# Attention and MLP on one core: the QKV lead as two streams of 64-row matmuls, with the sync queue in program order

## The chip, the cores and the metric

One core of a Trainium2 chip. The time is that of one launch of the whole program in device microseconds; before the change it is 1637.77 us, the median of three runs (1637.33 to 1638.07).

## The reference

One block of 2048 tokens, width 512, 32 heads of 16, and an MLP of width 1792. Everything is fp32, x has one batch.

```
xn = layernorm(x)                                   # no gain, no bias
q, k, v = split(xn @ wqkv)                          # 32 heads of 16
p  = softmax(q k^T / 4)                             # 2048 x 2048 for each head
s  = concat(p v) @ wo
g  = silu( relu(xn @ w1 + b1)^2 @ w2 + b2 )
return x + s * g
```

## The kernel before, in words

**Precision.** Each operand of a projection is held as a high and a low part, and each product is made of three matmuls, high by high, high by low and low by high (`terms3`, L270). A projection tile of 128 x 512 over a depth of 512 is therefore 12 matmuls: four slices of depth by three terms. A matmul that uses all 128 rows of the array is called full here. A matmul that uses rows 0 to 63 or 64 to 127 is called a half; two halves on different lanes (lane 0 the upper rows, lane 1 the lower ones) run side by side, as a pair. In the records a full matmul has the tile form 128*128 and a half has 64*128.

**Attention.** Heads go in quads, queries in chunks of 512: 8 quads by 4 chunks are 32 units. A unit has 16 blocks of 128 keys, so there are 512 slots. For each slot and each of four heads there is one half matmul of scores and one exponential (`exp_mm`, L1234 on PE and L1246 on ACT), and two slots later four matmuls of probabilities times values into one bank (`pv_mm`, L373). The exponential needs the row maximum, so a first pass computes the same scores with queries on the partitions and takes maxima (`max_mm`, matmul L298, VectorE reduction L305): 4 of these to a slot and 128 to a unit. They run 24 slots (LEAD) ahead of the exponentials. When a unit's maxima are done, `max_end` reduces them once more (L325), and `shift` (L333) turns, negates and splits them on VectorE (L335, L337, L338), stores them to HBM (`keep`, L344) and loads them into rows of the query tiles (`back`, `shift_rows`, L364), where the score matmul subtracts them.

**Lanes.** Heads 0 and 2 of a quad lie on lane 0, heads 1 and 3 on lane 1. The dense work of the MLP and of the output projection is cut into half matmuls too (`halves` L210, `block` L242), so that in the main loop each pair has one dense half on one lane and a maximum or a score on the other. A slot without dense work pairs maxima with scores.

**Start.** Up to 60 us, x is loaded, normalised, transposed and split, and the first projection tiles are made. From there a lead fills the 24 slots of advance with maxima: 48 rounds of one pair of maxima, and after every third pair two full projection tiles, 24 matmuls (`pump(24)`). `qk_tile` (L967) makes a tile of Q or K for eight heads and 512 tokens: 12 matmuls (L972), an evacuation by ACT into `raw` (L996, two buffers), a split by POOL into `hl` (L83 and L84, three buffers), and two stores of 256 KB by SP (L927). `v_tile` (L1011) makes V: matmuls L1019, ACT L1025, one store L1028. The tiles of the first eight heads (`m % 4 == 0`) are split by VectorE straight from the bank instead. The lead also stores the normalised x for the MLP (`xn_d`, L1221, eight stores of 1 MB on odd steps g below 16), and at g = 16 asks for the first MLP weights (L438), the values of quad 0 (L160) and the biases b1 and b2 (L1217, L1218).

**Banks.** PSUM has eight banks: three `se` (pool `pe`), three `pm_t` (pool `pm`), one `pd_t` and one `po`. Projection tiles of the lead alternate between `pd_t` and `po`.

**After the lead.** Slots 0 and 1 each do four maxima and four exponentials around the last projection tile, slots 2 and 3 do the same without it, and from slot 4 the dense work runs in groups of four slots (`long_slots`). The first of its operands is `xc` (L486), a load of 2 x 512 KB of normalised x that takes the place of the projection operands, so it is issued after the last projection matmul. Slots 452 and 453 lie between MLP and output projection and have no dense work; the maxima end with slot 487.

**What sets the order.** Up to the main loop ACT, VectorE and POOL run in program order; PE and SP are ordered by the scheduler of the tile framework. In the loop SP is in program order as well. A store or load deferred by `later(n, ...)` is issued n ticks later; in the loop a tick is a slot.

Of the kernel before, what the change touches and what calls it, by code (L numbers as in the profile page):

```python
# [36 lines left out]
GAPS = (18, 19, 20, 22)  # L37
EPS = 1e-5
# [3 lines left out]
def kernel(  # L42
# [56 lines left out]
    with ExitStack() as ph:  # L99
# [184 lines left out]
        togo = {}  # L284
# [4 lines left out]
        def max_mm(g, j, bank=None):  # L289
            u = g // 16  # L290
            qd = u // 4
            if u not in mxs:
                mxs[u] = sp.tile([P, 16, 4], F32, name="mx")
                for i in range(2):
                    togo[u, i] = [(p, qb, kc) for p in range(2) for qb in range(4) for kc in range(4)]
            p, qb, kc = togo[u, j].pop(0)
# [12 lines left out]
        def max_end(g):  # L309
            u, s = divmod(g, 16)  # L310
# [22 lines left out]
        def shift(u):  # L333
# [26 lines left out]
        in_loop = []  # L360
# [606 lines left out]
        def qk_tile(m, c, last=False):  # L967
            ps = pd.tile([P, 512], F32, name="pd_t") if last else qkv_bank()
# [9 lines left out]
            if last:  # L978

                hl = pools["n"].tile([P, 2, 512], F32R, name="hl")  # L980
                raw = sp.tile([P, 512], F32, name="ot", bufs=1)
                nc.scalar.activation(raw, ps, AF.Copy)
                split((hl[:, 0], hl[:, 1]), raw)
                later(6, lambda: qk_store(m, c, hl))
                yield
                return

            quick = m % 4 == 0 and not hold[0]

            def evac():  # L990
                hl = hlp.tile([P, 2, 512], F32R, name="hl")
                if quick:
                    split_psum(hl[:, 0], hl[:, 1], ps)
                else:
                    raw = hlp.tile([P, 512], F32, name="raw", bufs=2)
                    nc.scalar.activation(raw, ps, AF.Copy)  # L996
                    split((hl[:, 0], hl[:, 1]), raw)
                qk_store(m, c, hl)

            when_done(evac)  # L1000
            yield

# [8 lines left out]
        def v_tile(c, tt):  # L1011
            xT = xTs[c]
            ps = qkv_bank()
            ts_ = slice(tt * P, (tt + 1) * P)
            for out_, lh, rh, first_, last_ in terms3(ps, [
                (lambda a, q, ko=ko: xT[q, a, ko, ts_], lambda b, q, ko=ko: wa_t[q, b, ko, 2 * P :])
                for ko in range(KO)
            ]):
# [4 lines left out]
            def evac():  # L1023
                vt = vts[(4 * c + tt) % NVT]
                nc.scalar.activation(  # L1025
                    vt[:, :, :DH], ps.rearrange("p (h d) -> p h d", d=DH), AF.Copy
                )
                nc.sync.dma_start(v_d[:, c * 4 + tt, :], vt.rearrange("p h d -> p (h d)"))  # L1028

            when_done(evac)  # L1030
            yield
# [46 lines left out]
        rest = []  # L1078

# [10 lines left out]
        vts = [wqa.tile([P, H, VW], F32, name=f"vt{i}") for i in range(NVT)]  # L1090
        first = ExitStack()
# [20 lines left out]
        for i in range(NT + 3):  # L1112
# [38 lines left out]
            if i >= 7 and (i - 3) % 4 == 3:  # L1151
                c = (i - 3) // 4
                ahead.append(qk_tile(4, c))
                rest.append(qk_tile(0, c))
            if i >= 3 and (i - 3) % 4 == 3:
                c = (i - 3) // 4
                rest += [v_tile(c, tt) for tt in range(4)]
        let_go()
# [15 lines left out]
        for n in (2, 3):  # L1174
            fill_ring("ka", n, 1.0)
        rest += [
            qk_tile(m, c, (m, c) == (7, 3)) for c in range(4) for m in (1, 5, 2, 6, 3, 7)
        ]

        pump(47)  # L1180
        led.append(0)
        pump(24)
# [43 lines left out]
        def exp_mm(st, j, pts, spare):  # L1226
            u, kb = divmod(st, 16)
            qd = u // 4
            b = 64 * (j % 2)
            if spare:  # L1230
                se = pm.tile([P, 512], F32, name="pm_t")
            else:
                se = pe.tile([P, 512], F32, name="se")
            nc.tensor.matmul(  # L1234
                se, kas[qd, j // 2][b : b + 64, kb * P : (kb + 1) * P],
                qes[u][j // 2][b : b + 64, :],
                start=True, stop=True,
            )

            oldest_first("pt")  # L1240
# [223 lines left out]
```

## Time and profile before

| what | value |
|---|---|
| median of 3 runs | 1637.77 us |
| span of the profiled execution | 1635.6 us |
| time outside that span (median less span) | about 2.2 us |
| PE busy in it | 1620.8 us, 99% |
| VectorE, ACT, POOL busy | 1356.8, 1189.9, 523.0 us |
| the chain that ended last | PE 99%, VectorE 1% |

The page and the views of the trace give times in microseconds from the start of the span. A row of a timeline has the start, the length, the engine, the line of the kernel, the operation, what it writes and reads, how many instructions were put together in the row and, in brackets, how long its engine stood idle before it and what released it. PE is the matmul, PEld the load of its weights, and SPq the issue of a DMA on the queue of the sync engine SP. Matmuls overlap in the pipeline, so the distance between two starts is a matmul's cost, not the length in its row.

### The profile page before, as it was taken

To read this page: it belongs to the slowest core of one execution; us is meant where nothing else is said; L and a number is where in the kernel's file an instruction comes from. 1 tells how busy PE (TensorE), PEld (TensorE's weight loads), DVE (VectorE), ACT (ScalarE), POOL (GpSimd) and SP (SyncE) were. 2 spreads that over 40 slices of the span, in tenths; PEclk is the share of its full clock that TensorE was granted. 3 is DMA by queue.
4 is the path that set the end of the run, shared out by engine and by line. 5 is a ranking of instruction groups with operands and counts; after the bars stand their busy time and mean duration, and the time that the engine had idled before them with its cause. 6 is when DMAs were issued, how large, how long until landed. Compare 5 with 4: busy or idle time off the path is not lost.

```text
span 1635.6 us, 35352 instructions
## 1 busy us (share of the span) xinstructions
PE 1620.8 (99%) x13300; PEld 923.2 (56%) x13300; DVE 1356.8 (83%) x2345; ACT 1189.9 (73%) x2351; POOL 523.0 (32%) x547
## 2 busy tenths in 40 slices
PE   8999999999999999999999999999999999999998
PEld 6777565456546655664466456645654565445543
DVE  6356888888888888888888888888888888887754
ACT  7311777777777777877777777777777777777786
POOL 6446568123112311321133112311321233125421
PEclk9999999999999999999999999999999999999999
DMA  8768655434333333434343334323532353246654
GB/s 299 193 210 276 205 171 145 125 100 124 83 95 100 109 93 81 129 87 112 79 121 89 83 90 141 101 68 88 147 98 61 88 144 81 60 130 195 193 170 155
DMA packets 164418, 209.18 MB, mean 128 GB/s; under 512 B 59928, under 2 KB 78872, under 8 KB 162712
## 3 DMA queue, kind: packets, MB, share of 16 engines
q1 hardware_dynamic: 163960, 206.40, 44.5%
q8 instruction: 105, 1.72, 0.5%
q14 instruction: 65, 0.53, 0.1%
q10 hardware_dynamic: 288, 0.52, 0.1%
HBM read 149.95 MB, written 56.61 MB: 126 GB/s over the span
## 4 chain that ended last, share of the span: by engine, by line
PE 99%; DVE 1%; DMA 0%; issue 0%; ACT 0%; POOL 0%; DVEq 0%; POOLq 0%
PE po L373 31%; PE pd_t L242 18%; PE pm_t L298 18%; PE se L1234 15%; PE pd_t L210 6%; PE pd_t L972 2%; PE po L972 2%; PE se L1019 1%; PE se L972 1%; PE pd_t L1019 1%; PE se L298 1%; PE po L1019 1%; PE pm_t L1234 1%; PE pm_t L1065 0%; PE pm_t L811 0%; DVE mx L305 0%
## 5 line engine op out<-in xcount | busy, mean ns | idle before, releaser
L305 DVE TENSOR_REDUCE mx<-pm_t 128x1 f32<-128x512 f32 x2000 | 1245.1, 684 | 167.8 <-PE pm_t L298 77.3
L1246 ACT ACTIVATE pt<-se 128x512 f32<-128x512 f32 x2002 | 1044.2, 617 | 257.6 <-PE se L1234 214.5
L298 PE MATMUL pm_t<-ka,qm 64*128 64x512 f32 x2000 | 793.7, 420 | 1.5 <-DVE mx L305 1.3
L1234 PE MATMUL se<-qe,ka 64*128 64x512 f32 x2002 | 674.0, 396 | 0.2 <-ACT pt L1246 0.2
L373 PE MATMUL po<-pt,v 128*32 128x512 f32 x4096 | 545.3, 604 | 0.0
L298 PEld LDWEIGHTS pm_t<-ka,qm 64*128 64x128 f32 x2000 | 350.1, 184 | 244.8 <-DVE mx L305 230.7
L242 PEld LDWEIGHTS pd_t<-xc,w1s 64*128 64x128 f32 x2688 | 334.0, 187 | 93.9 <-issue 88.9
L242 PE MATMUL pd_t<-xc,w1s 64*128 64x256 f32 x2688 | 380.2, 288 | 0.0
L1234 PEld LDWEIGHTS se<-qe,ka 64*128 64x128 f32 x2002 | 337.6, 184 | 20.7 <-ACT pt L1246 2.6
L242 PE MATMUL pd_t<-w2t,hT 64*128 64x512 f32 x1080 | 300.6, 410 | 0.0
L242 PEld LDWEIGHTS pd_t<-w2t,hT 64*128 64x128 f32 x1080 | 179.1, 184 | 80.5 <-issue 75.5
L529 POOL TENSOR_TENSOR r<-r 128x512 f32<-128x512 f32 x56 | 58.2, 1040 | 374.9 <-ACT r L526 374.9
L373 PEld LDWEIGHTS po<-pt,v 128*32 128x32 f32 x4096 | 81.0, 108 | 158.8 <-issue 136.4
L548 POOL TENSOR_TENSOR u<-u,b_t 128x512 f32<-128x512 f32 x16 | 20.6, 1287 | 316.3 <-ACT u L547 316.3
L411 POOL TENSOR_TENSOR ot<-ot,hl 128x512 f32<-128x512 f32 x31 | 39.8, 1284 | 204.4 <-DMA hl<-r_d 91.1
L210 PE MATMUL pd_t<-wot,oc 64*128 64x512 f32 x336 | 90.9, 406 | 0.0
L526 ACT ACTIVATE r<-pd_t,b_t 128x256 f32<-128x256 f32 x112 | 46.9, 470 | 57.1 <-PE pd_t L242 57.1
L210 PEld LDWEIGHTS pd_t<-wot,oc 64*128 64x128 f32 x336 | 58.4, 184 | 45.4 <-ACT pt L1246 14.2
L84 POOL TENSOR_TENSOR hT<-r,hT 128x512 fp32r<-128x512 f32 x56 | 72.2, 1290 | 4.7
L210 PE MATMUL pd_t<-w2t,hT 64*128 64x512 f32 x264 | 68.8, 393 | 0.0
L305 DVE TENSOR_REDUCE mx<-se 128x1 f32<-128x512 f32 x48 | 32.9, 685 | 40.0 <-PE pm_t L298 30.0
L210 PEld LDWEIGHTS pd_t<-w2t,hT 64*128 64x128 f32 x264 | 47.0, 184 | 6.0
(129 smaller groups left out, 928.5 us busy)
## 6 DMA issues: line engine op xcount, KB each, us to landing
w1s<-w_d SPq DMA_DIRECT2D x196, 256.0 KB
qm<-q_d SPq DMA_DIRECT2D x384, 32.0 KB
ka<-k_d SPq DMA_DIRECT2D x96, 128.0 KB
qe<-q_d SPq DMA_DIRECT2D x384, 32.0 KB
xn_d<-xT SPq DMA_DIRECT2D x8, 1024.0 KB
k_d<-hl SPq DMA_DIRECT2D x32, 256.0 KB
q_d<-hl SPq DMA_DIRECT2D x32, 256.0 KB
xc<-xn_d SPq DMA_DIRECT2D x16, 512.0 KB
```

Source lines behind the costliest of these rows:

```text
L84: (lo or nc.gpsimd).tensor_tensor(dst[1], raw, dst[0].bitcast(F32), op=ALU.subtract)
L210: mm = nc.tensor.matmul(out_, lh(r), rh(r), start=first_ and lane == 0, stop=last_ and lane == 1, skip_group_check=True,)
L242: mm = nc.tensor.matmul(out_, lh(r), rh(r), start=first_ and lane == 0, stop=last_ and lane == 1, skip_group_check=True,)
L298: nc.tensor.matmul(ps, qms[u][p][64 * j : 64 * j + 64, qb * P : (qb + 1) * P], kas[qd, p][64 * j : 64 * j + 64, kc * 512 : (kc + 1) * 512] ...
L305: return nc.vector.tensor_reduce(mxs[u][:, c, kc : kc + 1], ps, axis=AX.X, op=ALU.max)
L373: nc.tensor.matmul(po[32 * j : 32 * j + 32, :], vs[qd][:, (4 * kb + j) * VW : (4 * kb + j) * VW + 32], pts[j], start=(kb == 0), stop=(kb = ...
L526: nc.scalar.activation(r[:, i], ps[:, i * CW : (i + 1) * CW], AF.Relu, bias=b1_t[:, fo : fo + 1])
L529: nc.gpsimd.tensor_tensor(r, r, r, op=ALU.mult)
L972: nc.tensor.matmul(out_[:, n0:n1], lh(slice(0, P)), rh(slice(0, P))[:, n0:n1], start=first_, stop=last_,)
L1019: nc.tensor.matmul(out_, lh(slice(0, P)), rh(slice(0, P)), start=first_, stop=last_)
L1234: nc.tensor.matmul(se, kas[qd, j // 2][b : b + 64, kb * P : (kb + 1) * P], qes[u][j // 2][b : b + 64, :], start=True, stop=True,)
L1246: return nc.scalar.activation(pts[j], se, AF.Exp, scale=0.25)
```

## The change

- The lead is rewritten (`side_tile`, `side_rounds`, `lead_rounds`). Tile v(2,0) is made full before it. The other 32 projection tiles are made of halves: 31 in sequence, each on lane 0 and, 18 rounds later, on lane 1 into the same bank, and tile (3,3) "across", on lane 1 in the first 18 rounds and on lane 0 in the last 18, so that both lanes are busy all the time. That is 390 rounds, and between them 60 extra pairs: 51 of two maxima, 9 of a maximum and a score. Six maxima on lane 1 at the head and three scores and three maxima on lane 0 at the tail fill the rest.
- The lead holds 120 maxima and 12 exponentials (slots 0, 1 and 2). Slots 0 and 1 are gone (FIRST = 2), slots 2, 3, 452 and 453 (TWO) hold two maxima each, and the maxima end before slot 486.
- Tiles of the lead lie in `pm_t`, and every fourth in `pd_t`; each bank comes up again four tiles later. All Q and K tiles but the across one go by ACT and POOL.
- SP is in program order in the lead. Stores of tiles are deferred by `later(1)` (V) and `later(2)` (Q, K), with a tick of six rounds; those of (7,3) go to the main loop.
- The stores of `xn_d` are on every third step g up to 23. The block at g = 16 is where it was.
- The loads of query tiles for maxima are asked for at steps 5 and 7 of a unit, not 9 and 11. A unit's last reduction follows the 64th maximum of a lane, and its shift is due six steps later.

```
+FIRST = 2
+LAST_MAX = 486
+TWO = (2, 3, 452, 453)
+ROUND_MM = [12 * k for k in range(1, 32)] + [12 * k + 6 for k in range(2, 22)]
+ROUND_MS = [12 * k + 6 for k in (22, 23, 25, 26, 28, 29)]
+ROUND_SM = [12 * k + 6 for k in (24, 27, 30)]
...
         def max_end(g):
+            for u in [u for u, n in left.items() if n == 0]:
+                del left[u]
+                m4 = m4s[u % 2]
+                nc.vector.tensor_reduce(m4[:, :16], mxs[u], axis=AX.X, op=ALU.max)
+                mxs[u] = m4
+                late.append((g + (6 if u else 2), u))
...
-            if s in (9, 11) and u + 1 < NU:
-                load_q_pair(u + 1, "qm", (s - 9) // 2, qms.setdefault(u + 1, []))
-            if s == 15:
-                assert not togo[u, 0] and not togo[u, 1]
-                m4 = m4s[u % 2]
-                nc.vector.tensor_reduce(m4[:, :16], mxs[u], axis=AX.X, op=ALU.max)
-                mxs[u] = m4
-                late.append((g + 2, u))
+            if s in (5, 7) and u + 1 < NU:
+                load_q_pair(u + 1, "qm", (s - 5) // 2, qms.setdefault(u + 1, []))
...
-            if in_loop:
-                later(1, keep)
-                later(2, back)
-            else:
-                keep()
-                back()
+            later(1, keep)
+            later(2, back)
...
+        def side_tile(spec, ps, end=None):
+            kind, a, b = spec
+            if kind == "v":
+                return v_terms(a, b, ps), lambda: v_done(a, b, ps, 1)
+            return qk_terms(a, b, ps), end or (lambda: qk_done(a, b, ps, False, 2))
+
+        def side_rounds(specs, single):
+            def half(tile_, lane, k):
+                terms, _, first = tile_
+                r = slice(64 * lane, 64 * lane + 64)
+                out_, lh, rh, first_, last_ = terms[k]
+                mm = nc.tensor.matmul(
+                    out_, lh(r), rh(r),
+                    start=first_ and lane == first, stop=last_ and lane != first,
+                    skip_group_check=True,
+                )
+                if k == 0 and lane != first:
+                    tc.add_manual_dep(
...
+            n, behind, count = 3 * KO, 3 * KO // 2, len(specs) - 1
+            (km, kc), tiles = specs[count][1:], {}
+            ps = pv.tile([P, 512], F32, name="po")
+            across = side_tile(specs[count], ps, lambda ps=ps: qk_done(km, kc, ps, True, 0)) + (1,)
+            extra = [0, 0]
+            for i in range(n * count + n + behind):
+                if i % n == 0 and i // n < count:
+                    k = i // n
+                    ps = pd.tile([P, 512], F32, name="pd_t") if k % 4 == 2 else pm.tile([P, 512], F32, name="pm_t")
...
+                for lane in range(2):
+                    at = i - (n + behind) * lane
+                    if 0 <= at < n * count:
+                        half(tiles[at // n], lane, at % n)
+                        if lane and at % n == n - 1:
+                            tiles.pop(at // n)[1]()
+                        continue
...
-        pump(24)
...
-        for rnd in range(2 * LEAD):
-            g = rnd // 2
-            if rnd % 2 == 0:
-                shift_due(g)
-            for j in range(2):
-                max_mm(g, j, None if j else lambda: pe.tile([P, 512], F32, name="se"))
-            if rnd % 3 == 2:
-                pump(24)
-            if rnd % 2 == 0:
-                continue
+        lead = ExitStack()
+        lead.enter_context(tc.manual_schedule(engines={mybir.EngineType.SP}))
...
+        def lead_rounds():
+            for i in side_rounds(specs, single):
+                if i % 6 == 0:
+                    now[0] = i // 6
+                    run_waiting()
+                kinds = "mm" if i in ROUND_MM else "ms" if i in ROUND_MS else "sm" if i in ROUND_SM else ""
+                uses = [single(lane, kind) for lane, kind in enumerate(kinds)]
...
+        rounds = lead_rounds()
+        for g in range(LEAD):
+            shift_due(g)
+            while min(made) < 2 * g + 2:
+                next(rounds)
             max_end(g)
...
-            if g % 2 and g < 16:
-                c, i = divmod(g // 2, 2)
+            if g % 3 == 2:
+                c, i = divmod(g // 3, 2)
                 nc.sync.dma_start(
                     xn_d[i, :, :, c * 512 : (c + 1) * 512], xTs[c][:, i].bitcast(F32)
                 )
+        for _ in rounds:
+            pass
+        run_waiting(True)
...
-        def slot(st, mms, post, fill=0):
+        def slot(st, mms, post):
...
-            spare = g >= NU * 16
+            spare = st >= LAST_MAX
...
+            if st in TWO:
+                for _ in range(2):
+                    max_mm(lane)
+                    ex.pop(0)()
+                if ex:
+                    kb, j = (kb0 + 1, 2 + lane) if lane else (kb0, lane)
+                    exp_mm(kb, j, pts[kb], True)
+                    ex.pop(0)()
+                last_use[0] = None
+                max_end(g)
+                return
```

More of the change, by code (lines that the diff above doesn't have):

```diff
@@ L1157 @@
                 rest += [v_tile(c, tt) for tt in range(4)]
+                order += [("v", c, tt) for tt in range(4)]
         let_go()
@@ L1223 @@
                 )
-        first.close()
[L1226 to L1240, printed above, removed]
-            n, pts[j] = next(
-                (n, t) for n, t in enumerate(rot["pt"])
-                if all(t is not x for d in pts_all.values() for x in d.values())
-            )
-            rot["pt"].append(rot["pt"].pop(n))
-            return nc.scalar.activation(pts[j], se, AF.Exp, scale=0.25)
+        for _ in rounds:
+            pass
+        run_waiting(True)
+        assert made == [60, 60] and not [1 for it in to_exp for _ in it]
+        lead.close()
+        first.close()
         pos = {}
@@ L1430 @@
             shift_due(st_ + 1 + LEAD)
-            if st_ > 1:
-                pv_step(st_ - 2, pts.pop(st_ - 2))
+            pv_step(st_ - 2, pts.pop(st_ - 2))
+        assert not [1 for it in stream for _ in it] and not left
         run_waiting(True)
```

199 lines of the change are left out of this document (133 added, 66 removed).

## The prediction

> **What bounds the kernel now.** I read the page first: its span, the busy times, the chain that ended last and the costliest groups.
>
> ```profile
> span 1635.6 us, 35352 instructions
> ...
> PE 1620.8 (99%) x13300; PEld 923.2 (56%) x13300; DVE 1356.8 (83%) x2345; ACT 1189.9 (73%) x2351; POOL 523.0 (32%) x547
> ...
> PE 99%; DVE 1%; DMA 0%; issue 0%; ACT 0%; POOL 0%; DVEq 0%; POOLq 0%
> ...
> L305 DVE TENSOR_REDUCE mx<-pm_t 128x1 f32<-128x512 f32 x2000 | 1245.1, 684 | 167.8 <-PE pm_t L298 77.3
> L1246 ACT ACTIVATE pt<-se 128x512 f32<-128x512 f32 x2002 | 1044.2, 617 | 257.6 <-PE se L1234 214.5
> ```
>
> TensorE is busy 99% of the span and is the chain. So a change can win only by giving PE less to do, and it loses whatever makes PE wait. The span is 1635.6; the median of the runs, 1637.77, lies 2.2 above it. The sums below are differences inside the span, put onto the median.
>
> The change acts on the lead and the slots behind it, so I took PE's timeline there, then pieces of it later that show the new forms of work.
>
> ```profile
> 60.54 0.49 PE L298 MATMUL se<-ka,qm 64*128 64x512 f32 x1
> ...
> 61.43 3.05 PE L1019 MATMUL pd_t<-wa_t,xT 128*128 128x512 f32 x12
> 64.31 2.96 PE L1019 MATMUL po<-wa_t,xT 128*128 128x512 f32 x12
> 67.20 0.50 PE L298 MATMUL se<-ka,qm 64*128 64x512 f32 x1
> ```
>
> ```profile
> 165.94 0.50 PE L298 MATMUL pm_t<-ka,qm 64*128 64x512 f32 x1
> ...
> 169.89 1.67 PE L972 MATMUL pd_t<-xT,wr_t 128*128 128x512 f32 x6
> ...
> 178.08 0.50 PE L298 MATMUL pm_t<-ka,qm 64*128 64x512 f32 x1
> 178.12 0.47 PE L242 MATMUL pd_t<-xc,w1s 64*128 64x256 f32 x2
> ...
> 181.66 0.49 PE L298 MATMUL pm_t<-ka,qm 64*128 64x512 f32 x1
> ```
>
> ```profile
> 1553.01 0.39 PE L210 MATMUL pd_t<-wot,oc 64*128 64x512 f32 x1
> ...
> 1554.41 0.62 PE L210 MATMUL pd_t<-wot,oc 64*128 64x512 f32 x2
> ...
> 1582.02 0.50 PE L1234 MATMUL pm_t<-qe,ka 64*128 64x512 f32 x1
> ...
> 1583.68 0.50 PE L210 MATMUL pd_t<-wot,oc 64*128 64x512 f32 x1
> ```
>
> The reader is to see four prices. A full tile of 12 matmuls is 64.31 - 61.43 = 2.88. A run of dense halves beside scores and maxima takes (1554.41 - 1553.01)/6 = 0.233 a pair, so 12 full matmuls cost as much as 12.3 pairs. Three pairs of maxima between full tiles take 61.43 - 60.54 = 0.89 and not 0.70: a turn from full to half and back costs 0.19. And a slot of two pairs with its values takes 1.66. No engine makes PE wait in the lead: the window over it has PE at 106.0 of 106.
>
> ```profile
> 60.00:166.00 106.00, 106.00 (x485) 78.91 (x483) 61.74 (x102) 22.28 (x38) 52.22 (x60) 1.00 0.72 238
> ```
>
> That row has VectorE at 61.74, ACT at 22.28, POOL at 52.22 and the DMA engines at 0.72. PE never waits there, but the chain from tile to HBM (ACT, POOL, SP, DMA) is already well used.
>
> **The change, part by part.**
>
> *The lead's own work.* From the first maximum at 60.54 to the first pair with MLP work at 178.08 the kernel before takes 117.54. The new lead does a full tile (2.88), a turn (0.19) and 390 + 60 = 450 pairs (450 x 0.233 = 105.0), and then slots 2 and 3 at 1.66 each: 111.4 in all, if nothing waits. The gain is **-6.1**. It comes from 16 turns that go, from slots 0 and 1, and from maxima and scores that ride beside projection halves.
>
> *The first MLP load.* This is seen in SP's queue and in the DMA engines' slices.
>
> ```profile
> 136.42 1.60 SPq L438 DMA_DIRECT2D ex<-in_B_w_dram  x3
> 138.07 0.59 SPq L160 DMA_DIRECT2D v<-v_d  x1
> 138.71 3.32 SPq L1217 DMA_DIRECT2D b_t<-in_B_b_dram  x1
> 142.07 1.99 SPq L1218 DMA_DIRECT2D b_t<-in_B_b_dram  x1
> 144.15 0.38 SPq L344 DMA_DIRECT2D sh_d<-sh  x1
> 144.63 0.85 SPq L927 DMA_DIRECT2D k_d<-hl  x2
> 145.57 0.45 SPq L927 DMA_DIRECT2D q_d<-hl  x1
> 147.57 2.24 SPq L364 DMA_DIRECT2D qe<-sh_d  x4
> ...
> 167.46 1.69 SPq L927 DMA_DIRECT2D q_d<-hl  x2
> 169.19 2.73 SPq L137 DMA_DIRECT2D qe<-q_d  x6
> 172.03 1.25 SPq L486 DMA_DIRECT2D xc<-xn_d  x2
> ```
>
> ```profile
> DMA  9382113402889999999974003345212144260054
> ```
>
> The slices run from 170 to 184 us, 0.35 each; the busy stretch of the 1 MB of xc ends with the 22nd, at 177.7. So xc needs 177.7 - 172.03 = 5.7 from its issue. It takes the projection operands' place and cannot be asked for before the last of those matmuls. Before, that one ends at 169.89 + 1.67 = 171.6, and the 6.5 us to 178.08 are filled by eight maxima that wait for VectorE and two slots of values; xc is just in time. After, the last projection half is in the last round, and only slots 2 and 3 (3.3) stand behind it. If xc is issued 0.4 behind it (172.03 - 171.6), PE waits 0.4 + 5.7 - 3.3 = 2.8; with a pair of stores in front on SP, which is in program order, 1.69 more, 4.5. I take **+3.8**. VectorE's backlog in slots 2 and 3 lies inside this wait and costs nothing of its own.
>
> *SP in program order, the block at g = 16.* The rows from 136.42 to 147.57 are the block: three weights 1.60, values 0.59, b1 3.32, b2 1.99, `keep` 0.38, a wait for what it stored (147.57 - 144.53 = 3.04), `back` 2.24, together 13.2. Before, the scheduler put three stores into the gap ahead of `back`. In the new program order no store of Q or K stands between the weights and the end of `back`. A tile comes every 12 rounds and two extra pairs, 14 x 0.233 = 3.27, so four tiles finish meanwhile, and the first of them, due two ticks (12 rounds) after its matmuls, is stored some 13.2 - 3.3 = 10 late. What that does is visible in small in POOL's timeline.
>
> ```profile
> 148.99 0.62 POOL L83 TENSOR_SCALAR hl<-raw 128x512 fp32r<-128x512 f32 x1 [2.09 <-DMA k_d<-hl]
> 149.69 1.29 POOL L84 TENSOR_TENSOR hl<-raw,hl 128x512 fp32r<-128x512 f32 x1
> ```
>
> POOL stood 2.09 for a buffer that the store of 144.63 gave back, 148.99 - 145.48 = 3.5 after its issue. `hl` has three buffers, so one comes round every 3 x 3.27 = 9.8, of which the split takes 1.99, the planned delay leaves 0.7 more, the issue takes 0.85 and the landing 3.5: slack is 2.8, and POOL gets 10 - 2.8 = 7 late. `raw` has two buffers: 6.5 between uses, less 0.6 for the copy and 1.99, so ACT gets 7 - 4 = 3 late. ACT runs in order, and behind its copies are now the lead's exponentials, whose `se` banks are the maxima's as well; PE waits when three are full. That is 3, between 0 (all absorbed by banks) and 5 (the late stores meet three xn_d stores of 1 MB, which before were through by then).
>
> *The query loads at g = 23.* There `max_end` asks for 12 loads at once (qe and qm; six take 2.73, so 5.5), an xn_d store behind them, then the tile stores. By the same chain they are 5.5 + 0.5 late on a queue that has just worked off the block: 2.5, between 0.5 and 4.
>
> *The first exponentials.* They stand at round 270, close to where `back` lands, behind the 13.2: 1.0, between 0 and 2. The three are **+6.5** together, from 0.5 to 11.
>
> [...]
>
> *Shifts.* Their reductions stay, but they move.
>
> ```profile
> L337 DVE TENSOR_SCALAR sh<-tr 128x32 fp32r<-128x32 f32 x32 | 8.3, 258 | 1.1
> ...
> L335 DVE STREAM_TRANSPOSE tr<-m 128x32 f32<-128x32 f32 x32 | 6.5, 202 | 0.0
> L338 DVE SCALAR_TENSOR_TENSOR sh<-tr,sh 128x32 fp32r<-128x32 f32 x32 | 6.4, 200 | 1.1
> ```
>
> The 0.66 of a shift used to fall behind slot 8 of each 16 and now falls behind slot 11, ahead of a slot with five maxima: five at 0.684 are 3.42 of its 181.66 - 178.08 = 3.58. The spare of 0.16 is taken once a unit; three banks hide part. For some 29 units 0 to 4.6; I take 0.07 each, **+2.0**. The query loads four slots sooner cost nothing: in the loop SP is far from full, and the ring's third tile is free by then.
>
> *The later slots.*
>
> ```profile
> 1455.18 0.50 PE L298 MATMUL pm_t<-ka,qm 64*128 64x512 f32 x1
> ...
> 1460.61 0.50 PE L298 MATMUL pm_t<-ka,qm 64*128 64x512 f32 x1
> ...
> 1565.83 0.50 PE L298 MATMUL pm_t<-ka,qm 64*128 64x512 f32 x1
> ...
> 1574.46 0.50 PE L210 MATMUL pd_t<-wot,oc 64*128 64x512 f32 x1
> ```
>
> Slots 452 and 453 take 5.43 and become two of 1.66: at most -2.1; their neighbours keep VectorE busy, so -1.3. Slots 486 to 488 take 8.63; without maxima they go at the pace of 12 exponentials, 12 x 0.617 = 7.4, so -1.3 (down to -2.9 if exponentials overlap more). Together **-2.6**.
>
> *The sum.* -6.1 + 3.8 + 6.5 + 2.0 - 2.6 = +3.6, so 1637.77 + 3.6 = 1641.4.
>
> **The rivals.**
>
> *Faster: the lead does not wait.* If the late stores cost only buffers, the 6.5 shrinks to 0.5 and xc's wait to 2.8: -6.1 + 2.8 + 0.5 + 1.0 - 2.6 = -4.4, 1633.4. For it: in the window PE did not wait once although POOL stood 2.09. Against it: that store was 3.5 behind its issue and not 10 late. It decides when the first store after the block is less than 2.8 + 4 = 6.8 late. Chance 0.20.
>
> *No difference.* The lead waits by half, 3.2: +0.3, 1638.1. For it: ACT has only 22.28 of 106 to do and catches up fast, and nine of twelve exponentials are spread one to a tile. Against it: the second burst at g = 23 comes before the first is worked off. Chance 0.28.
>
> *The DMA engines are the bound.* They are at 0.72 over the lead, the work of the lead is pressed into less time, and three xn_d stores move to its last third. Then the lead waits 9 to 11 and the sum is +6 to +8, 1645. Chance 0.14.
>
> *The streams do not run as pairs.* If halves of projections on both lanes cost 0.25 and not 0.233, 390 x 0.017 = 6.6 are lost and it is 1648. Against it: L242 and L210 beside maxima show 0.233. Chance 0.03.
>
> **How the numbers follow.** The forecast has the remaining 0.35 and is the likeliest; its own range is 1640 to 1643.5. This kernel's measurement tells 0.2%, 3.3 us, from no change: 1634.5 to 1641.05. Below it lies the first rival, 0.20; inside it the second and the lower edge of the forecast, 0.28 + 0.05 = 0.33; above it 0.47. The range runs from the first rival to the DMA case, 1632.5 to 1646.5, and leaves out the fourth and the ends of the unknown costs.
>
> **What would show each step.** Pairs in the lead 0.233 apart and the stretch from the first maximum to the first MLP half near 111.4 plus 10: right. A wait of PE before the first L252 matmul, released by the DMA of xc, of 3 to 4.5. In SP's queue a stretch of 13 from weights to the end of `back` with no store of Q or K, then POOL waiting for DMA of `hl` by up to 7, ACT's copies waiting for POOL, and PE for exponentials in `se`, from about 140 to 170. Slots 452 and 453 at 1.7 to 2.1 each, slots 486 to 488 at 2.3 to 2.5. The steps between units longer by 0.07. The prediction is wrong if PE shows no idle rows between 140 and 165, or if the loop's units change by more than 0.16 each.

## The result, and the profile after

The changed kernel takes 1664.28 us (median of four runs, 1662.71 to 1667.6) against 1637.77: 26.5 us more, a ratio of 1.0164 with a 95% interval of 1.0150 to 1.0179. The forecast was 3.6 more. The profiled execution has a span of 1662.4, 26.8 above that of before.

The page of the changed kernel has its span and the chain that ended last.

```profile
span 1662.4 us, 36155 instructions
...
PE 93%; DMA 3%; DVE 2%; SPq 1%; issue 1%; POOL 1%; ACT 0%; POOLq 0%; DVEq 0%; ACTq 0%
```

The chain was 99% PE and is 93%: DMA, VectorE, SP and POOL now hold the end back. What PE waited for is in the view of waits (total, times, longest). Before the change none of these rows was over 1.3 in total. `oc` is the operand of the output projection, loaded from `on_d`.

```profile
PE se L314 <- ACT pt L1195: 7.2, 2, 5.1
...
PE pm_t L314 <- DVE mx L321: 5.2, 8, 0.9
PE pd_t L220 <- DMA oc<-on_d: 4.0, 1, 4.0
PE pd_t L252 <- DMA xc<-xn_d: 3.2, 2, 1.9
...
PE se L1183 <- DVE mx L321: 0.8, 1, 0.8
```

Where the loss arises is read from the first values matmul of a slot, which exists in both kernels. The rows of slots 4, 451, 453, 485 and 489, before and then after:

```profile
180.66 1.06 PE L373 MATMUL po<-pt,v 128*32 128x512 f32 x8
...
1454.18 1.06 PE L373 MATMUL po<-pt,v 128*32 128x512 f32 x8
...
1459.59 1.07 PE L373 MATMUL po<-pt,v 128*32 128x512 f32 x8
...
1564.83 1.06 PE L373 MATMUL po<-pt,v 128*32 128x512 f32 x8
...
1575.36 1.07 PE L373 MATMUL po<-pt,v 128*32 128x512 f32 x8
```

```profile
193.67 1.12 PE L384 MATMUL po<-pt,v 128*32 128x512 f32 x8
...
1478.39 1.06 PE L384 MATMUL po<-pt,v 128*32 128x512 f32 x8
...
1482.53 1.06 PE L384 MATMUL po<-pt,v 128*32 128x512 f32 x8
...
1593.62 1.07 PE L384 MATMUL po<-pt,v 128*32 128x512 f32 x8
...
1602.20 1.06 PE L384 MATMUL po<-pt,v 128*32 128x512 f32 x8
```

The distances are 13.0, 24.2, 22.9, 28.8 and 26.8 us. So the lead and its first MLP load cost 13.0, the units of the main loop 11.2 (below this growth is called the drift), slots 452 and 453 give back 1.3, the output projection loses 5.9, and the slots without maxima give back 2.0.

**The lead.** Its rows on PE, in order of time:

```profile
147.98 0.49 PE L314 MATMUL se<-ka,qm 64*128 64x512 f32 x1 [2.07 <-ACT pt L1195]
...
174.51 0.79 PE L314 MATMUL se<-ka,qm 64*128 64x512 f32 x1 [5.08 <-ACT pt L1195]
...
175.10 0.62 PE L1061 MATMUL pm_t<-xT,wr_t 64*128 64x512 f32 x1
...
175.53 0.62 PE L1061 MATMUL pm_t<-xT,wr_t 64*128 64x512 f32 x1
...
181.15 0.62 PE L1061 MATMUL pd_t<-xT,wr_t 64*128 64x512 f32 x2
...
188.10 0.35 PE L252 MATMUL pd_t<-xc,w1s 64*128 64x256 f32 x1 [1.85 <-DMA xc<-xn_d]
189.81 0.38 PE L252 MATMUL pd_t<-xc,w1s 64*128 64x256 f32 x1 [1.36 <-DMA xc<-xn_d]
```

PE waits 2.07 and 5.08 for exponentials, then 1.85 and 1.36 for xc, and behind the second wait the pairs are 175.53 - 175.10 = 0.43 apart and not 0.233. The windows show why (the columns after the five engines are the granted clock, the DMA share and GB/s):

```profile
137.50:143.00 5.50, 5.46 (x48) 5.34 (x50) 2.27 (x5) 1.30 (x3) 2.57 (x4) 1.00 0.93 339
148.00:154.00 6.00, 6.00 (x38) 4.89 (x40) 2.27 (x4) 1.08 (x2) 3.77 (x4) 0.72 1.03 380
174.50:180.50 6.00, 5.99 (x30) 4.67 (x32) 0.69 (x1) 1.06 (x2) 4.40 (x5) 0.53 0.54 201
```

The granted clock of TensorE is 1.00 ahead of the first wait, 0.72 over the 6 us behind it and 0.53 behind the second. Over 6 us these are 6 x 0.28 = 1.7 and 6 x 0.47 = 2.8 us lost behind the two waits.

Behind ACT stood POOL, and behind POOL the stores. ACT's copies ahead of the two exponentials, then SP's queue, then POOL, in the changed kernel:

```profile
146.84 0.60 ACT L1000 ACTIVATE raw<-pd_t 128x512 f32<-128x512 f32 x1 [3.45 <-POOL hl L94]
...
173.37 0.60 ACT L1000 ACTIVATE raw<-pm_t 128x512 f32<-128x512 f32 x1 [7.58 <-POOL hl L94]
```

```profile
123.92 1.57 SPq L449 DMA_DIRECT2D ex<-in_B_w_dram  x3
...
134.86 2.23 SPq L375 DMA_DIRECT2D qe<-sh_d  x4
137.19 0.83 SPq L938 DMA_DIRECT2D q_d<-hl  x2
...
158.69 3.16 SPq L147 DMA_DIRECT2D qe<-q_d  x6
161.95 3.30 SPq L147 DMA_DIRECT2D qm<-q_d  x6
165.29 0.53 SPq L1355 DMA_DIRECT2D xn_d<-xT  x1
```

```profile
140.26 0.63 POOL L93 TENSOR_SCALAR hl<-raw 128x512 fp32r<-128x512 f32 x1 [6.00 <-DMA q_d<-hl]
...
171.37 0.62 POOL L93 TENSOR_SCALAR hl<-raw 128x512 fp32r<-128x512 f32 x1 [7.64 <-DMA k_d<-hl]
```

From 123.92 to 137.19 no store of Q or K is issued, 13.3 us, and POOL waits 6.00 for the buffer of the store at 137.19. At g = 23 SP issues 12 query loads and a store of 1 MB, from 158.69 to 165.82, and POOL waits 7.64. The chain of the prediction is there link by link, the second one larger than the first.

**The units.** In most units the slot behind slot 11 is longer. The usual loss is about 0.27; units 3, 10, 17 and 24 lose 1.28, units 0 to 2 lose 0.7 to 1.0, and a few lose nothing. VectorE and PE in unit 10:

```profile
675.86 0.20 DVE L353 TENSOR_SCALAR sh<-tr 128x32 fp32r<-128x32 f32 x1
676.09 1.22 DVE L354 SCALAR_TENSOR_TENSOR sh<-tr,sh 128x32 fp32r<-128x32 f32 x1
677.23 3.07 DVE L321 TENSOR_REDUCE mx<-pm_t 128x1 f32<-128x512 f32 x5
```

```profile
677.97 0.50 PE L314 MATMUL pm_t<-ka,qm 64*128 64x512 f32 x1 [0.90 <-DVE mx L321]
```

The last of the shift's three operations (the second row here) took 1.22 and not 0.19, and the five reductions of the next slot start behind it. What POOL did at that moment is told at the end.

### The profile page after: what moved, and what is told of

The parts are those of the page before. It is cut to its first block, busy times and chain, and to the rows that moved or that the text cites. A ratio compares the mean times of both kernels' runs of the same rounds, so it can differ in the third digit from the quotient of the medians.

```text
span 1662.4 us, 36155 instructions
## 1 busy us (share of the span) xinstructions
PE 1628.7 (98%) x13684; PEld 939.1 (56%) x13684; DVE 1363.0 (82%) x2346; ACT 1192.8 (72%) x2351; POOL 524.7 (32%) x547
## 4 chain that ended last, share of the span: by engine, by line
PE 93%; DMA 3%; DVE 2%; SPq 1%; issue 1%; POOL 1%; ACT 0%; POOLq 0%; DVEq 0%; ACTq 0%
PE po L384 30%; PE pd_t L252 18%; PE pm_t L314 17%; PE se L1183 14%; PE pd_t L220 5%; PE pm_t L1061 3%; PE se L1031 1%; PE se L983 1%; DVE mx L321 1%; PE pd_t L1061 1%; DMA q_d<-hl 1%; PE se L314 1%; DMA xr<-in_A_x_dram 1%; SPq L147 1%; PE pm_t L1183 1%
## 5 line engine op out<-in xcount | busy, mean ns | idle before, releaser
L321 DVE TENSOR_REDUCE mx<-pm_t 128x1 f32<-128x512 f32 x1931 | 1199.7, 684 | 182.6 <-PE pm_t L314 90.3
L314 PE MATMUL pm_t<-ka,qm 64*128 64x512 f32 x1931 | 775.7, 422 | 5.3 <-DVE mx L321 5.2
L314 PEld LDWEIGHTS pm_t<-ka,qm 64*128 64x128 f32 x1931 | 339.6, 184 | 249.6 <-DVE mx L321 234.8
L252 PE MATMUL pd_t<-xc,w1s 64*128 64x256 f32 x2688 | 386.3, 290 | 3.2 <-DMA xc<-xn_d 3.2
L252 PEld LDWEIGHTS pd_t<-w2t,hT 64*128 64x128 f32 x1080 | 178.9, 184 | 81.9 <-issue 75.5
L321 DVE TENSOR_REDUCE mx<-se 128x1 f32<-128x512 f32 x117 | 76.0, 687 | 36.6 <-PE se L314 27.8
L1061 PE MATMUL pm_t<-xT,wr_t 64*128 64x512 f32 x408 | 77.1, 400 | 0.0
```

Source lines behind the costliest of these rows:

```text
L252: mm = nc.tensor.matmul(out_, lh(r), rh(r), start=first_ and lane == 0, stop=last_ and lane == 1, skip_group_check=True,)
L314: nc.tensor.matmul(ps, qms[u][p][64 * j : 64 * j + 64, qb * P : (qb + 1) * P], kas[qd, p][64 * j : 64 * j + 64, kc * 512 : (kc + 1) * 512] ...
L321: return nc.vector.tensor_reduce(mxs[u][:, c, kc : kc + 1], ps, axis=AX.X, op=ALU.max)
L1061: mm = nc.tensor.matmul(out_, lh(r), rh(r), start=first_ and lane == first, stop=last_ and lane != first, skip_group_check=True,)
```

## The experiments

Times are medians; "on before" is the ratio to the kernel before with its interval.

**One number of the shift** (e_shift3).

```
-                late.append((g + (6 if u else 2), u))
+                late.append((g + (3 if u else 2), u))
```

> The changed kernel with one number changed: shifts are due three steps after the last maximum and not six, so they fall behind slot 8 of a unit, after the slot with five maxima. Theory A (the 0.66 us of a shift on VectorE just ahead of that slot is what each unit loses): the steps of 0.27 a unit and the four of 1.28 behind slot 11 vanish, that is 9 to 11 us, and SP's wait of 7.2 us for the stored shift at 1505 us moves to another place, so the 4 us wait for oc shrinks too: 1664.3 goes to 1645 to 1655. Rival B (the units lose time to the earlier query loads on SP or to the lead's backlog): the steps stay and the time is within 2 us of 1664.3.

Measured: 1656.79, on before 1.0111 (1.0095 to 1.0128). The first values matmul of slot 4 is 13.7 behind that of before, of slot 6 14.5, and that of slot 406 still 14.5: of the 11 us of drift nothing is left. Theory A holds for the units, and its number is just missed. The lead varies by a microsecond or two between executions (13.0 in the changed kernel, 14.5 here and 12.8 in the next one, all with the same lead). The wait for oc did not shrink, against theory A: it moved to slot 462 (4.10), and the output projection lost 8.4 where it had lost 5.9.

**The distance of the shift** (e_shift5). The same with 5 in place of 6.

> The changed kernel with shifts due five steps after the last maximum, behind slot 10 of a unit instead of slot 11 (six steps) or 8 (three). Theory A (what matters is whether a slot with five maxima or one with three follows): slot 11 has three, so the units lose nothing, as in e_shift3, 9 to 11 us less than 1664.3. Rival B (the distance to slot 8 matters, an earlier shift is better): half of the drift stays, 4 to 7 us less.

Measured: 1655.46, 1.0104 (1.0088 to 1.0119), 8.8 less. The steps of 0.27 are gone, so for them it counts that a slot of three maxima follows, not an early shift, as theory A says. Its number is not reached in the units: of the drift 4.4 is left at slot 406 and 5.8 at slot 451, so the units give back 5.4. Of what is left 2.7 is one wait for a POOL split of w2 in unit 2, 1.2 a step in unit 27, the rest steps of about 0.5. Another 3.1 of the 8.8 come from the output projection. The wait for oc is 1.33 here, where it was 3.98 with 6 steps and 4.10 with 3: a first sign that it hangs on the shift.

**SP in the lead** (e_sp_sched).

```
-        lead.enter_context(tc.manual_schedule(engines={mybir.EngineType.SP}))
```

> The changed kernel with SP left to the scheduler in the lead, as before the change; all else the same. Theory A (program order on SP is what makes the lead wait): the scheduler puts tile stores into the gaps of the block and ahead of the query loads, so PE waits in the lead fall from 8 us to under 3, with the slower pairs behind them: 6 to 12 us faster. Rival B (DMA load or the buffers alone): under 3 us.

Measured: 1657.03, 1.0117 (1.0102 to 1.0133), 7.3 less. PE's waits in the lead are now these two:

```profile
124.50 0.79 PE L1061 MATMUL pd_t<-xT,wr_t 64*128 64x512 f32 x1 [2.55 <-ACT raw L1000]
...
149.58 0.50 PE L314 MATMUL se<-ka,qm 64*128 64x512 f32 x1 [0.81 <-ACT pt L1195]
```

The slot-4 distance falls from 13.0 to 5.7, while the drift and the wait for oc stay as they were. Program order on SP is worth 7.3 of the 13.0. Theory A.

**The biases ahead of the lead** (e_bias). The loads of b1 and b2 move from g = 16 to g = 0.

```
+            if g == 0:
+                nc.sync.dma_start(b1_t, b1.rearrange("(fo p) -> p fo", p=P), allow_slow_non_contiguous=True)
+                nc.sync.dma_start(b2_t, b2[None, :].to_broadcast([P, D]))
...
-                nc.sync.dma_start(b1_t, b1.rearrange("(fo p) -> p fo", p=P), allow_slow_non_contiguous=True)
-                nc.sync.dma_start(b2_t, b2[None, :].to_broadcast([P, D]))
```

> The changed kernel with the loads of b1 and b2 asked for at g = 0 and not at g = 16, so SP's block without tile stores is 5.2 us shorter; the bytes are the same. Theory A (SP in program order delays the stores, which hold hl, then POOL, ACT and PE): POOL's wait of 6.0 us at 140 falls to about 1, the PE waits of 0.8 and 2.07 us in the lead vanish with the slower pairs behind the second (2.2), and the 5.08 at 174 stays: 3 to 6 us faster than 1664.3. Rival B (the DMA engines, nine tenths busy there, are the bound and the stores land late anyway): within 1.5 us of 1664.3.

Measured: 1662.64, 1.0154 (1.0138 to 1.0169), 1.6 less, which is B's number. Part of A is seen: POOL's first wait falls from 6.0 to 4.2, PE's from 0.80 and 2.07 to 1.49 and 0.41, and the slower pairs behind it go (granted clock 1.00 from 145.7 to 152). Two things eat the rest. SP's stretch without tile stores is 11.5 and was 13.3, so only 1.8 of the 5.2 come back: the store of the shift takes 3.25 to issue and took 1.45, and its loads then stand 3.45 for its landing and stood 1.85. And the wait at g = 23 grows from 5.08 to 6.35: a stream that comes sooner to the same late store waits there. How much of the first is B's full DMA engines this run does not separate.

**The stores of xn_d at their old steps** (e_xn).

```
-            if g % 3 == 2:
-                c, i = divmod(g // 3, 2)
+            if g % 2 and g < 16:
+                c, i = divmod(g // 2, 2)
```

> The changed kernel with the eight 1 MB stores of xn_d on odd steps below 16, as before the change, so none of them competes in the last third of the lead; SP's order is otherwise the same. Theory A (SP's order): the waits of POOL at 140 and 171 shrink by less than 2 us and the time falls by 0 to 3. Rival B (DMA load): stores land sooner, both waits go, and the time falls by 7 to 12.

Measured: 1663.49, 1.0157 (1.0141 to 1.0172), with runs from 1659.93 to 1666.24: about a microsecond less, inside the spread. In its profile the slot-4 distance is 9.5, 3.5 less: PE now waits 5.13 for the loads behind the first shift and 0.53 for exponentials. The output projection loses 8.9 there and not 5.9, which takes most of it back. POOL's waits are neither theory's, 8.32 in place of 6.00 and 5.28 in place of 7.64. So the stores' place moves the waits and has a share in the lead, up to 3.5 by one profile, which the medians do not show.

**The query loads at their old steps** (e_shift3_q), on top of the shift by 3.

```
-            if s in (5, 7) and u + 1 < NU:
-                load_q_pair(u + 1, "qm", (s - 5) // 2, qms.setdefault(u + 1, []))
+            if s in (9, 11) and u + 1 < NU:
+                load_q_pair(u + 1, "qm", (s - 9) // 2, qms.setdefault(u + 1, []))
```

> The kernel of e_shift3 with the query loads for maxima at steps 9 and 11 of a unit, as before the change. Theory A (the earlier loads put 12 issues, some 6 us, ahead of oc on SP, so the first output-projection work waits for oc): PE's waits for oc (4.1 and 1.1 us) go, with the slower pairs behind them, 5 to 7 us faster than e_shift3's 1656.8, and no unit waits for its queries. Rival B (oc is late because slots 452 and 453 are shorter, or because the DMA engines are full there): the waits stay, the time is within 1.5 us. Rival C (the maxima now run four slots further ahead and need the loads sooner): PE waits for qm in most units, several us slower.

Measured: 1658.35, 1.0126 (1.0111 to 1.0142), nothing gained over 1656.79. PE waits 2.42 and 2.89 for query tiles in the first four units and up to 0.35 later, as rival C has it, and the waits for oc shrink to 2.19 and 1.48 and stay. The earlier loads are needed, since the maxima now run further ahead.

**All four together** (e_all: shift 3, queries at 9 and 11, SP scheduled, biases early).

> The changed kernel with shifts three steps after the last maximum, query loads at steps 9 and 11, SP left to the scheduler in the lead, and b1 and b2 loaded at g = 0. If the parts add up (shift 11, SP's order 7, biases 1 to 2, oc 6), 26 of the 26.9 us come back and it is within 2 us of the kernel before, at 1637 to 1641; the wait for xc, 6 us with the slower pairs, is what eats the gain of the halves. If they overlap (the same stores late for another reason), 1641 to 1648.

Measured: 1652.71, 1.0091 (1.0076 to 1.0106). The parts did not add up: PE waits for query tiles again, 1.79 at slot 4 and 2.94, 0.90 and 0.28 in the units. The drift is 9.0, where it is 0.6 without the later loads (next run).

**Without the later queries** (e_lead: shift 3, SP scheduled, biases early).

> The changed kernel with shifts three steps after the last maximum, SP left to the scheduler in the lead and b1 and b2 at g = 0: e_all without the later query loads. Theory A (the waits for qm in e_all, 1.8, 2.9 and smaller ones, come from the later loads): they go, 6 to 10 us faster than e_all's 1652.7, at 1643 to 1647. Rival B: they come from the lead's backlog and stay, 1650 to 1653.

Measured: 1646.15, 1.0047 (1.0032 to 1.0062), 6.6 less than with them. Theory A. Three edits return 18.1 of the 26.5.

**Four pairs of maxima from the lead into slots 2 and 3** (e_fill, e_best).

```
-ROUND_MM = [12 * k for k in range(1, 32)] + [12 * k + 6 for k in range(2, 22)]
+ROUND_MM = [12 * k for k in range(1, 32)] + [12 * k + 6 for k in range(2, 18)]
...
             if st in TWO:
...
+                if st < 4:
+                    for _ in range(2):
+                        max_mm(lane)
+                        max_mm(1 - lane)
```

On top of the shift by 3:

> The kernel of e_shift3 with four pairs of maxima taken out of the lead and put into slots 2 and 3, behind the last projection matmul. Theory A (the stretch between that matmul and the MLP is bound by the load of xc, whatever PE does in it): the four pairs go into the wait for nothing, the lead is 0.9 shorter, the wait for xc shrinks from 3.4 us to under 1, the slower pairs behind it go: 1.5 to 3 us faster than e_shift3. Rival B (VectorE, which then has 12 maxima in these two slots, 7.2 us, becomes the bound): 0 to 2 us slower.

Measured: 1656.59, 1.0113 (1.0096 to 1.0130), nothing. The wait for xc is gone, but PE waits 8.34 for VectorE at 180.30: there VectorE stands behind the split of the across tile, which stands behind an ACT copy that waits 8.31 for a buffer held by a store. So the late stores behind g = 23 had found another way, and neither theory is shown. On top of the last kernel, where those stores are not late:

> The kernel of e_lead with four pairs of maxima moved from the lead into slots 2 and 3, behind the last projection matmul and inside the wait for xc. With the lead's late stores gone, theory A (the wait for xc is a fixed time from the last projection matmul) has 1 to 3 us off e_lead; rival B (VectorE binds slots 2 and 3) 0 to 2 us on it.

Measured: 1647.33, 1.0052 (1.0037 to 1.0067), against 1646.15: no difference that the runs can tell, though in the profile no wait for xc is left and slot 4 is 4.2 behind before and not 4.9. The profile shows what took the place of the wait. VectorE's row, and the stretch behind it at half the granted clock:

```profile
171.95 5.46 DVE L321 TENSOR_REDUCE mx<-pm_t 128x1 f32<-128x512 f32 x9
```

```profile
175.95:179.36 3.41, 3.41 (x14) 1.03 (x13) 1.95 (x4) 0.46 (x1) 2.63 (x5) 0.50 0.97 302
```

Nine reductions follow each other without a gap, PE's extra maxima have no partner and stand about 0.6 apart, VectorE's pace, and 3.41 us run at half the clock. That is rival B's mechanism, and it costs nearly what the wait for xc had cost.

**The price of a wait of PE** (e_clock). The kernel before, with extra reductions on VectorE ahead of seven slots.

```
+IDLE = {104: 3, 136: 4, 168: 5, 200: 6, 232: 8, 264: 10, 296: 14}
...
             begin(st_)
+            for _ in range(IDLE.get(st_, 0)):
+                nc.vector.tensor_reduce(seen, b2_t, axis=AX.X, op=ALU.max)
```

> The kernel before the change with 3, 4, 5, 6, 8, 10 and 14 extra reductions of 0.6 us on VectorE ahead of slots 104, 136, 168, 200, 232, 264 and 296, so that PE waits for rising lengths. Theory A (a wait of PE over some length, between 1 and 2 us, is followed by 4 to 6 us in which pairs are 0.427 apart and not 0.233): the short waits cost their own length, the long ones 2 to 3 us more, and the granted clock shows it. Rival B (the slower pairs in the changed kernel come from its lead, not from the wait): every stop costs its own length.

Measured: 1682.97, 1.0275 (1.0255 to 1.0296). The second, third and fourth of the seven waits, and the windows behind them:

```profile
561.22 0.49 PE L299 MATMUL pm_t<-ka,qm 64*128 64x512 f32 x1 [2.31 <-DVE mx L306]
...
655.63 0.50 PE L299 MATMUL pm_t<-ka,qm 64*128 64x512 f32 x1 [3.05 <-DVE mx L306]
752.43 0.79 PE L299 MATMUL pm_t<-ka,qm 64*128 64x512 f32 x1 [3.77 <-DVE mx L306]
```

```profile
561.20:567.00 5.80, 5.78 (x55) 3.55 (x57) 5.54 (x12) 3.35 (x7) 0.00 (x0) 1.00 0.08 22
655.60:661.00 5.40, 5.37 (x32) 1.98 (x32) 3.89 (x9) 1.80 (x4) 0.00 (x0) 0.68 0.06 13
752.40:758.00 5.60, 5.57 (x24) 2.52 (x24) 3.73 (x9) 1.21 (x3) 0.00 (x0) 0.50 0.06 19
```

The slots behind grew by 1.74, 2.68, 4.93 and 6.75 us for waits of 1.36, 2.31, 3.05 and 3.77: 0.4 above the wait for the first two, 1.9 and 3.0 for the others. Waits of 5.19, 6.65 and 9.51 cost 2.9, 2.2 and 2.0 above themselves. So the five waits of 3.05 and more cost 1.9 to 3.0 us above themselves, also in the kernel before: theory A, though its limit of 1 to 2 us is too low for the 2.31, which cost 0.4 above itself here with the clock at 1.00. In the lead of the changed kernel 2.07 had the half clock behind it (0.72 over 6 us), so length alone does not tell the two apart.

**Slots 452 and 453 at four maxima again** (e_two), on top of the shift by 3.

```
-TWO = (2, 3, 452, 453)
-ROUND_MM = [12 * k for k in range(1, 32)] + [12 * k + 6 for k in range(2, 22)]
+TWO = (2, 3)
+ROUND_MM = [12 * k for k in range(1, 32)] + [12 * k + 6 for k in range(2, 20)]
...
-            order = "s" * len(ex) if spare else {0: "smsmsmsm", 1: "smsmssm"}[k]
+            order = "s" * len(ex) if spare or k == 4 else {0: "smsmsmsm", 1: "smsmssm"}[k]
```

> The kernel of e_shift3 with slots 452 and 453 at four maxima each again; two pairs of maxima fewer in the lead pay for them. Theory A (the output projection waits for oc because PE comes to it sooner, through the shorter slots 452 and 453 and a unit whose maxima end earlier): the wait of 4.1 us near slot 462 falls to under 2, and the time is about equal to e_shift3, as the shorter slots' gain is what was lost again. Rival B (SP gets to oc later for another reason): the wait stays at 4 and the kernel is 1 to 2 us slower than e_shift3's 1656.8.

Measured: 1654.71, 1.0100 (1.0084 to 1.0117). The wait for oc is 2.66 and was 4.10: the shorter slots explain about the 1.3 by which PE comes sooner, no more, which lies between the theories. Its gain of 2 us over the shift alone is in the lead (9.0 at slot 4, where it was 13.7), where the other split of pairs moved the waits.

**What holds oc.** In the changed kernel SP stores the shift of unit 29 at 1504.97 and then stands 7.2 until it has landed, with everything else behind it (SP's rows, then SP's view of waits):

```profile
1504.97 0.62 SPq L360 DMA_DIRECT2D sh_d<-sh  x1
1512.92 2.11 SPq L375 DMA_DIRECT2D qe<-sh_d  x4
...
1537.31 0.78 SPq L667 DMA_DIRECT2D oc<-on_d  x1
```

```profile
SPq L375 <- DMA sh_d<-sh: 40.6, 29, 7.2
```

Two kernels on top of e_lead (1646.15) move only the end of the program, and a third joins both with the four pairs. The shift of unit 29 two steps later (e_tail_s):

```
-                late.append((g + (3 if u else 2), u))
+                late.append((g + ((5 if u == 29 else 3) if u else 2), u))
```

> The kernel of e_lead (1646.2, a wait of 3.1 us for oc near slot 462) with the shift of unit 29 alone two steps later, where it was before the change in relation to the weights of the output projection. Theory A (the loads of the shifted values wait on SP for their store, with the oc loads behind them in program order): the wait for oc near slot 462 goes or falls under 1, 3 to 5 us faster. Rival B (the query loads of unit 31, four slots sooner, hold the oc loads): unchanged, within 1 us.

Measured: 1643.34, 1.0035 (1.0024 to 1.0046), 2.8 less, just under theory A's 3 to 5. The wait of 3.1 at slot 462 is gone; waits for oc of 1.39 at 1519.55 and 1.99 at 1594.92 remain.

The query loads of unit 31 alone at the old steps (e_tail_q):

```
-            if s in (5, 7) and u + 1 < NU:
-                load_q_pair(u + 1, "qm", (s - 5) // 2, qms.setdefault(u + 1, []))
+            s0 = 9 if u == 30 else 5
+            if s in (s0, s0 + 2) and u + 1 < NU:
+                load_q_pair(u + 1, "qm", (s - s0) // 2, qms.setdefault(u + 1, []))
```

> The kernel of e_lead with the query loads of unit 31 alone at steps 9 and 11, as before the change. Theory A (shift): within 1 us of e_lead and the wait at slot 462 stays at 3. Rival B (query loads): the wait goes, 3 to 5 us faster.

Measured: 1647.86, 1.0058 (1.0043 to 1.0073), and the wait at slot 462 is 3.33. For this wait it is the shift, not the queries. Both, with the four pairs in slots 2 and 3 (e_tail_sq):

> Both of these, with the four pairs of maxima in slots 2 and 3 as in e_best. If each holds some of the oc loads, no wait for oc over 0.5 us is left and the kernel is at 1640 to 1643; if a third cause (the full DMA engines) holds them, the wait stays at 2 to 3 and it is at 1644 to 1647.

Measured: 1642.47, 1.0025 (1.0012 to 1.0037), with runs from 1637.76 to 1646.75. The waits for oc are 0.82 and 0.86, nearer to the first expectation, and the time is in its range. Its median is the lowest of these kernels, though its runs overlap those of e_tail_s, and still above before. What is left in its profile is the lead, 5.7 at slot 4, and here too the filled slots run at half the clock (0.50 from 174.42 to 184.66).

## Why the prediction was wrong

The direction was right, the size was not: a range up to 1646.5 against 1664.3. By its steps:

*The lead's own work, -6.1.* Right. The pairs are 0.233 apart where nothing waits, and the full tile, 450 pairs and slot 3 add up as stated; slot 2 took some 0.8 more, for VectorE, ahead of the wait for xc and within that term. The lead began 0.76 later (its full tile at 61.30, the first maximum of before at 60.54), which I had left out.

*SP's block, the query loads, the first exponentials, +6.5.* The mechanism was right and seen at each link, and one line undid 7.3 of the 13.0 at slot 4. The waits are 2.07 (I had 3), 5.08 (2.5) and 0.80 (1.0), 8.0 in all. The row of the 0.80 names VectorE as its releaser; in e_shift3, with the same lead, the same wait (1.27) ends with the loads of the shift. What failed is that I priced a wait of PE at its length. Pairs behind two of these waits ran at half the clock (means of 0.72 and 0.53 over 6 us), some 4 more, so the lead lost 12.2 (from 61.30 to 181.6, less the 108.1 of its work). The trace of before could not show this: PE never waited there.

*xc, +3.8.* The waits are 1.85 and 1.36, with a granted clock of 0.50 behind them (190.5 to 193): from the last projection half (181.6) to the values of slot 4 (193.67) 12.1 passed, where 3.3 + 2.6 (180.66 - 178.08) were the floor, so 6.2.

These four give 0.76 - 6.1 + 12.2 + 6.2 = 13.1 of the measured 13.0.

*Shifts, +2.0.* Measured: 11.2, the largest miss. The place (VectorE, ahead of the slot with five maxima) was named and is shown by moving it, but I took 0.07 from a range of 0 to 0.16 a unit, reasoning that the banks would hide part of the 0.66. Banks and spare took 0.4 of it and left 0.27 in the usual unit. The upper end was wrong too: it was the slot's spare, but what a unit can lose is the shift less the spare, 0.50, and in four units the last operation of the shift, beside a POOL product, took a microsecond longer (1.22 and not 0.19).

*Later slots, -2.6.* 1.3 for slots 452 and 453, as forecast, and 2.0 for the slots without maxima, where I had 1.3.

*The output projection* was not in the sum at all: 5.9. Shift and query loads were priced on VectorE and dismissed on SP ("SP is far from full"); there the store and the loads of a shift with a landing between them stop a queue in program order, and in the one place where weights and oc load as well this reached PE. Of the 5.9 the wait for oc is 4.0; behind it the granted clock was 0.50 for 3.4 us (1542.05 to 1545.5), some 1.7 more. To count what is queued behind a wait on SP was done for the lead and not here.

None of the rivals gives 1664. The nearest in kind, DMA as the bound of the lead, is not excluded as a part of it: moving the stores of 1 MB gave the lead 3.5 in one profile, SP's order 7.3, and the DMA share around the first wait was 0.93 to 1.03. The two were not separated.

What is left of the lead has a place. With SP scheduled, shifts and biases moved, slot 4 is still 3.4 to 5.7 behind before, with a wait for xc of 3.5 to 4 us and slower pairs behind it (0.43 apart in e_lead and e_tail_s) or, where four pairs of maxima fill that wait, without one. Filling it gains nothing in the medians because the filled slots go at VectorE's pace and at half the granted clock: for 3.41 us in e_best and for 10.24 in e_tail_sq, where that alone can be up to 5.1 of the 5.7. This is read from the two profiles; no run changed it.

## What to carry to other kernels

Work that is moved keeps its cost but meets other neighbours: look, on each engine and queue that it uses, at what comes right behind the new place, and take the operation's length less the spare there, not the spare, as the upper end. A queue in program order with a store, a wait for its landing and loads behind it must have nothing urgent queued after (here SP stood up to 7.2 us for such a landing, and PE 3.98 for the oc queued behind). And a stop of PE can cost more than its length: in e_clock those of 3.05 to 9.51 us cost 1.9 to 3.0 more and those of 1.36 and 2.31 cost 0.4 more, and behind one of 2.07 in the changed kernel the clock was at half for 3.41 us. Put such a surcharge on a long stop, as an estimate, until a trace shows that it was cheaper.

## What the runs showed of the hardware

Some waits of TensorE cost more than themselves. In e_clock the mean granted clock was 1.00 over 5.50 us behind the wait of 1.36 and over 5.80 behind that of 2.31, 0.68 over 5.40 behind 3.05 and 0.50 over 5.60 behind 3.77. In the lead of the changed kernel it was 0.72 over 6 us behind 2.07 and 0.53 over 6 us behind 5.08. The half clock behind the 2.07 lasted 3.41 us; the first of these rows holds most of the wait, the second the half clock, the third what came after:

```profile
146.05:149.46 3.41, 1.48 (x12) 1.26 (x14) 1.31 (x2) 1.08 (x2) 0.96 (x2) 1.00 0.99 349
149.46:152.87 3.41, 3.41 (x18) 2.71 (x16) 0.69 (x1) 1.08 (x2) 3.24 (x4) 0.50 1.05 406
152.87:156.28 3.41, 3.41 (x32) 2.81 (x30) 1.98 (x3) 1.09 (x2) 0.32 (x1) 1.00 0.64 224
```

The waits of 2.07 and 2.31 are close in length, and the clock was halved behind the shorter one alone. What decides this is not shown: no run placed a wait on purpose to test it. In the filled slots of e_best and e_tail_sq the clock was at 0.50 too, for 3.41 and 10.24 us, and in e_best PE was busy in all of the 3.41.

In four units of the changed kernel a VectorE operation took longer, and no row says what for. In unit 10 the subtraction of the shift starts at 676.09, just behind the start of a POOL product at 675.97, and ends at 677.31 with it (675.97 + 1.29 = 677.26); units 3, 17 and 24 show the same, with 1.22 each. This is POOL's row:

```profile
675.97 1.29 POOL L422 TENSOR_TENSOR ot<-ot,hl 128x512 f32<-128x512 f32 x1
```

The same operation takes 0.19 in the usual unit. In e_shift3, where the shift falls elsewhere, the operation takes about 0.19 in these four units; in e_shift5 it takes 1.25, 0.57 and 0.48 in units 27, 6 and 13, each time ending with a POOL operation that had started just before. That VectorE stood for POOL there is the author's reading of these rows; no run moved POOL's operation alone.
